# Sixteen-byte offsets for the operands of the matmuls

## The chip, the cores and the metric

The kernel runs on one core of a Trainium2 chip. The metric is the device time of one execution in microseconds. Three runs of the kernel before took 460.17 us in the median (460.16 to 460.78).

## The reference

Inputs are float32 q, k, v of shape (2, 12, 448, 64) and float64 weights, which arrive as pairs of 32-bit words. Cut to what is computed:

```python
scores = q @ k.transpose(0, 1, 3, 2) / sqrt(64)          # causal mask, softmax
x = (softmax(scores) @ v) -> (896, 768)                  # 2 batches x 448 tokens, 12 heads x 64
h = x @ w_in                                             # 768 -> 1024
solu = h * softmax(h)
y = layernorm(solu) * g_ln @ w_out                       # 1024 -> 768
out = relu(y @ moe2_w_in) ** 2 @ moe2_w_out              # 768 -> 2048 -> 768
```

## The kernel before

Every large product runs on TensorE in fp32r, with each operand split into a rounded part ("hi") and the remainder ("lo"); a product is three matmuls, hi x hi, hi x lo and lo x hi. TensorE loads 128 columns of one operand as weights (the second argument of `nc.tensor.matmul`) and streams the columns of the other (the third). The argument order in the listing is output, weights, moving operand; the profile prints the two inputs in either order.

The work is in five stages. Attention (to about 93 us, with a tail of L358 to 116 us) works head pair by head pair; its `pv` (L358) multiplies in plain fp32, with 448 and 64 or 320 and 192 columns, and one such matmul of the code shows as two instructions in the profile. Then h = x w_in (`h_part`, L474): for each of 7 token tiles and 6 channel blocks c, weights from x (`xT[c][s]`), moving operand from `W1[c]`, 512 columns. Then the layer norm, with transposes (L599), and y (`y_part`, L621): weights from `WO[fi]`, moving operand from `lnT`, for fi 0 to 7. Its first part (`y0`, order fi, then channel pairs cp) streams 384 columns; the second (`y1`, order cp, then fi) streams 512. For one fi and one cp there are 6 matmuls. Then y w_in2 (L752): weights from `W2[fi]`, moving operand from `yT[c][s]` in halves of 448 columns, 16 blocks of 36 matmuls. Last, the output product (L781): weights from `G[fi][s]`, moving operand from `W2[n]`, 384 columns, 16 blocks of 42 matmuls (two fi by 7 token tiles by 3).

The tiles that the change touches: `xT` and `yT` are the same 12 buffers (`xy_tiles`, L102, tags xy00 to xy51, c 0 to 5 and s 0 for hi, 1 for lo), 896 floats a partition. The output tiles `o` (L792) use 7 of those tags again. `G` (L719) is 32 tiles of 896 floats, for fi 0 to 15 and s 0 and 1. The weight buffers are handed out by `load_w` (L117) and `parts` (L127). `load_w` takes a buffer of a tag (w0, w1, w2 in one pool for blocks n modulo 3; the same three tags in a second pool, `wst`; wo0 to wo5 for `WO`) and loads the raw 64-bit words into it. `as_f32` (L139, three DVE instructions, L149 to L151) turns them into a float32 tile, and `parts` takes the same buffer again for hi (ACT, L674 in the last stages) and lo (POOL, L677). Three blocks ahead is loaded, two ahead is split: at the end of block n the load of block n+3 goes out, into the buffer that block n has freed.

The order of the work on each engine is written out by hand in `SEQ` for the stages up to y and by the loops from L747 on for the rest.

Where the buffers lie: every row length of these tiles is a multiple of 64 bytes (3584, 8192, 6144). In the compiled program all buffers of xy, w0 to w2 and `wst` begin at a multiple of 64 bytes within a partition; `lnT`, wo0 to wo5 and all of G begin 32 bytes past one. The slices that the matmuls take begin at multiples of 64 bytes within their tiles. So `WO[6]` and `WO[7]`, which lie in `wst`, begin at 0 modulo 64, and `WO[0]` to `WO[5]` at 32.

Of the kernel before, what the change touches and what calls it, by code (L numbers as in the profile page):

```python
# [7 lines left out]
F32 = mybir.dt.float32  # L8
F32R = mybir.dt.float32r
I32 = mybir.dt.int32  # L10
# [49 lines left out]
def attention_moe_kernel(tc, kq, v, w_in, w_out, g_ln, w_in2, w_out2, out):  # L60
# [7 lines left out]
    NP, P, _, S = kq.shape  # L68
    D = P // 2
    NT, DM = out.shape  # L70
# [5 lines left out]
    NF2 = DFF2 // P  # L76
# [7 lines left out]
    def pool(name, bufs=1, side="left", space=None):  # L84
        kw = {"space": space} if space is not None else {}
        return tc.tile_pool(name=name, bufs=bufs, side=side, reuse_waits="tile", **kw)

    def f(ap):
        return ap.bitcast(F32)

    with es:
        const = es.enter_context(pool("const"))
        xy = es.enter_context(pool("xy"))
# [5 lines left out]
        nhalf = const.tile([P, 1], F32, name="nhalf")  # L99
        nc.gpsimd.memset(nhalf, -0.5)  # L100

        def xy_tiles(nm):  # L102
            return [
                [xy.tile([P, NT], F32R, tag=f"xy{c}{s}", name=f"{nm}{c}{s}") for s in range(2)]
                for c in range(NC)
            ]

        xT = xy_tiles("xT")

        stage = ExitStack()  # L110
# [3 lines left out]

        wide = w_in.dtype != F32

        def load_w(pl, tag, src, W=2 * DFF, part=False):  # L117

            n = src.shape[1] if len(src.shape) < 3 + wide else src.shape[1] * src.shape[2]
            t = pl.tile([P, W], I32 if wide else F32, tag=tag, name="raw")  # L120
            d = t[:, 0 : 2 * n].rearrange("p (f t) -> p f t", t=2) if wide else t[:, 0:n]
            dd = d.rearrange("p (c f) ... -> p c f ...", c=src.shape[1]) if len(src.shape) > len(d.shape) else d
            if not part:
                nc.sync.dma_start(dd, src)
            return pl, tag, d, W

        def parts(w):  # L127

            pl, tag, d, W = w
            n = d.shape[1]  # L130
            t = pl.tile([P, W], F32R, tag=tag, name="w")
            return t[:, 0 : 2 * n].rearrange("p (s f) -> p s f", s=2)

        def words(w):
# [27 lines left out]
        def bank2(nm):  # L162

            pl = slots.pop(0)
            t = pl.tile([P, 2, 512], F32, tag="b", name=nm)
            slot_of[id(t)] = (pl, t)
            return t

        def give(t):
            slots.append(slot_of.pop(id(t))[0])  # L170
# [5 lines left out]
        with att:  # L176
# [7 lines left out]
            raw = qk_.enter_context(pool("raw", bufs=3, side="right"))  # L184
# [263 lines left out]
            def load_w1(c):  # L448
                W1[c] = load_w(w0 if c < 3 else wst, f"w{c % 3}", w_in[c * P : c * P + P, :])

            def load_w1_part(p):

                c, j = divmod(p, 4)
                src = w_in[c * P : c * P + P, :]
                if j == 0:
                    W1[c] = load_w(w0, f"w{c % 3}", src, part=True)
                n = DFF // 4
                nc.sync.dma_start(W1[c][2][:, n * j : n * j + n], src[:, n * j : n * j + n])
# [4 lines left out]
            def w1_hi(c):  # L463
                W1[c] = parts(W1[c])
                nc.scalar.copy(W1[c][:, 0], w_f[c])
# [71 lines left out]
            def load_wo(fi):  # L537
                pl, tag, W = (M["lnp"], f"wo{fi}", 2 * DM) if fi < NWO else (wst, f"w{fi - NWO}", 2 * DFF)
                WO[fi] = load_w(pl, tag, w_out[fi * P : fi * P + P, :], W)
# [4 lines left out]
            def wo_hi(fi):  # L544
                WO[fi] = parts(WO[fi])
                nc.scalar.mul(WO[fi][:, 0], w_f["o", fi], g_sb[:, fi : fi + 1])
# [95 lines left out]
            def y_out(cp, a):  # L642
                if not yT:
                    yT.extend(xy_tiles("yT"))
                b = (YB, YB1)[a].pop(cp)
                o, n = CH0 * a, (CH0, CH1)[a]
                for ci in range(2):
                    hi, lo = yT[2 * cp + ci]
                    nc.scalar.copy(hi[:, o : o + n], b[:, ci, 0:n])  # L649
                    nc.vector.tensor_tensor(lo[:, o : o + n], b[:, ci, 0:n], f(hi[:, o : o + n]), ALU.subtract)  # L650
                give(b)
# [20 lines left out]
            def w2_hi(n):  # L672
                W2[n] = parts(W2[n])
                nc.scalar.copy(W2[n][:, 0], w_f["2", n])  # L674
# [41 lines left out]
            moe0.close()  # L716
            gp = m2.enter_context(pool("gp", side="right"))
            tm = m2.enter_context(pool("tm", bufs=2))
            G = [[gp.tile([P, NT], F32R, name=f"g{fi}{s}") for s in range(2)] for fi in range(NF2)]  # L719
            HT = NT // 2  # L720
            rl = {}
            hb = {}
# [2 lines left out]
            def next_w2(n):  # L725

                if n + AHEAD < N2:
                    w2_f(n + AHEAD)
                    w2_hi(n + AHEAD)
                    w2_lo(n + AHEAD)  # L730
                if n + 3 < N2 and n + 3 >= NL2:
                    load_w2(n + 3)

            def relu_sq(fi):
# [4 lines left out]
                give(b)  # L739
                nc.scalar.copy(G[fi][0], rl[fi].rearrange("p a n -> p (a n)"))  # L740

            def relu_lo(fi):
                nc.vector.tensor_tensor(
                    G[fi][1], rl.pop(fi).rearrange("p a n -> p (a n)"), f(G[fi][0]), ALU.subtract
                )
# [21 lines left out]
            os_ = []  # L767
            for n in range(NF2, N2):
                half, fi = blocks2[n]
                if fi == 0:  # L770
                    bs = []
                last = fi == NF2 - TL
                for e, t in [(e, t) for t in range(NTT) for e in range(TL)] if last else [
                    (e, t) for e in range(TL) for t in range(NTT)
                ]:
                    if fi + e == 0 and t % 2 == 0:
                        bs.append(bank2("o"))
                    ob = bs[t // 2][:, t % 2, 0:HD]
                    hi, lo = (W2[n][:, s, HD * e : HD * e + HD] for s in range(2))
                    for s, w, r in ((0, hi, 0), (0, lo, 1), (1, hi, 2)):  # L780
                        nc.tensor.matmul(  # L781
                            ob,
                            G[fi + e][s][:, P * t : P * t + P],
                            w,
                            start=(fi + e == 0 and r == 0),
                            stop=(fi + e == NF2 - 1 and r == 2),
                        )
                    if not (last and e == TL - 1):
                        continue

                    if half == 0:
                        os_.append(xy.tile([P, NT], F32, tag=f"xy{t // 2}{t % 2}", name="o"))  # L792
                    if t % 2 or t == NTT - 1:
                        for t_ in range(t - t % 2, t + 1):
                            o = os_[t_][:, HD * half : HD * half + HD]
                            (nc.vector.tensor_copy if t_ % 2 else nc.scalar.copy)(o, bs[t // 2][:, t_ % 2, 0:HD])
                            nc.sync.dma_start(out[P * t_ : P * t_ + P, HD * half : HD * half + HD], o)
                        give(bs[t // 2])
                next_w2(n)
# [38 lines left out]
```

## Time and profile before

| What | us |
|---|---|
| Median of three runs | 460.17 |
| Span of the profiled execution | 459.8 |
| PE busy (matmuls) | 452.7 |
| PEld busy (weight loads) | 402.0 |
| DVE busy | 275.1 |
| ACT busy | 164.6 |
| POOL busy | 120.8 |

The span runs from the first to the last instruction of the profiled execution. A time of its own for that execution, from outside, is not among the runs listed; the runs give 460.16 to 460.78. PE and PEld are the two halves of TensorE, matmuls and loads of weights, and overlap. Matmuls are pipelined: an instruction lasts longer than the step to the next one, so the pace is the length of a block over its count, not the mean duration.

### The profile page before, as it was taken

Reading aid. Unit: us, or ns where it says so; the run is one execution under the profiler, and the core shown is the slowest. Engines: PE = TensorE matmul, PEld = TensorE weight load, DVE = VectorE, ACT = ScalarE, POOL = GpSimd, SP = SyncE. Lnnn points to the kernel's source line nnn. Section 1 sums busy time; section 2 is a strip of 40 time slices with the busy share of each in tenths; the row PEclk is TensorE's granted clock in tenths of the full one; section 3 lists DMA queues with packets and bytes.
Section 4 is the critical chain, followed back from the end, with each engine's and each line's share of the span. In section 5 each row is a group of like instructions: output and inputs, shape, how many; then the busy total and the mean of one; then the engine's idle time right before and its main releaser. Section 6 shows DMA issues by size and latency. Waiting matters only on the chain.

```text
span 459.8 us, 6525 instructions
## 1 busy us (share of the span) xinstructions
PE 452.7 (98%) x2535; PEld 402.0 (87%) x2535; DVE 275.1 (60%) x524; ACT 164.6 (36%) x213; POOL 120.8 (26%) x122
## 2 busy tenths in 40 slices
PE   8999899999999999999999999999999999999996
PEld 6777676787888899988899999999999999999996
DVE  8889687857569998741346566665763334342321
ACT  3465565533566636231133333424331010310101
POOL 3124547355321011110021322313122231222210
PEclk9999999999999999999999999999999999999999
DMA  8357765232173360000042423324243342734313
GB/s 251 128 154 221 207 159 164 62 79 98 41 280 133 96 248 2 0 1 0 0 138 69 138 80 127 116 91 137 70 137 80 128 113 94 240 90 135 86 52 120
DMA packets 41689, 52.47 MB, mean 114 GB/s; under 512 B 18234, under 2 KB 32314, under 8 KB 41274
## 3 DMA queue, kind: packets, MB, share of 16 engines
q1 hardware_dynamic: 41658, 52.05, 37.1%
q8 instruction: 20, 0.33, 0.3%
q14 instruction: 11, 0.09, 0.1%
HBM read 49.16 MB, written 2.80 MB: 113 GB/s over the span
## 4 chain that ended last, share of the span: by engine, by line
PE 93%; DMA 1%; POOL 1%; ACT 0%; issue 0%; SPq 0%; ACTq 0%; POOLq 0%
PE h L752 25%; PE o L781 25%; PE y L621 13%; PE h L474 13%; PE U L358 9%; PE s L317 4%; PE mxp L257 1%; DMA bc<-d 1%; PE T L599 1%; PE s L325 1%; POOL x L399 1%; PE mxp L284 0%; PE s L333 0%; ACT PP L349 0%; SPq L301 0%
## 5 line engine op out<-in xcount | busy, mean ns | idle before, releaser
L752 PE MATMUL h<-yT,w 128*128 128x448 f32 x576 | 116.9, 365 | 0.0
L781 PE MATMUL o<-w,g 128*128 128x384 f32 x672 | 116.8, 336 | 0.0
L781 PEld LDWEIGHTS o<-w,g 128*128 128x128 f32 x672 | 116.5, 188 | 0.3 <-DVE relu L738 0.2
L752 PEld LDWEIGHTS h<-yT,w 128*128 128x128 f32 x576 | 108.2, 188 | 8.6
L677 POOL TENSOR_TENSOR w<-wf,w 128x768 fp32r<-128x768 f32 x32 | 59.4, 1856 | 206.2 <-ACT w L674 206.2
L149 DVE TENSOR_SCALAR wf<-raw 128x768 int32<-128x768 int32 (+1 forms) x46 | 26.3, 573 | 83.6 <-DMA raw<-in_moe_w_out_dram 58.2
L674 ACT CAST w<-wf 128x768 fp32r<-128x768 f32 x32 | 26.8, 838 | 137.7 <-DVE wf L151 99.4
L474 PE MATMUL h<-w,xT 128*128 128x512 f32 x252 | 59.5, 393 | 0.0
L621 PE MATMUL y<-lnT,w 128*128 128x384 f32 (+1 forms) x288 | 58.9, 365 | 0.0
L621 PEld LDWEIGHTS y<-lnT,w 128*128 128x128 f32 x288 | 51.9, 188 | 5.9
L474 PEld LDWEIGHTS h<-w,xT 128*128 128x128 f32 x252 | 46.8, 188 | 9.6
L358 PE MATMUL U<-PP,VR 128*128 128x448 f32 (+1 forms) x192 | 49.2, 400 | 0.1
L151 DVE SCALAR_TENSOR_TENSOR wf<-raw,wf 128x768 int32<-128x768 int32 (+1 forms) x46 | 47.3, 1029 | 1.6
L150 DVE SCALAR_TENSOR_TENSOR wf<-raw,wf 128x768 int32<-128x768 int32 (+1 forms) x46 | 47.2, 1027 | 1.6
L358 PEld LDWEIGHTS U<-PP,VR 128*128 128x128 f32 x192 | 32.1, 190 | 16.4 <-issue 11.1
L399 POOL TENSOR_TENSOR x<-E,bc 64x448 f32<-64x448 f32 x24 | 31.9, 1328 | 47.2 <-DMA bc<-d 42.7
L272 DVE CUSTOM_DVE_ANT_0 JK<-mxp,MK 112x336 bf16<-112x336 f32 (+2 forms) x96 | 38.8, 446 | 8.5 <-PE mxp L257 7.5
L349 ACT ACTIVATE PP<-s 128x1024 f32<-128x1024 f32 x24 | 24.5, 1023 | 12.9 <-PE s L325 7.2
L738 DVE TENSOR_TENSOR relu<-h,relu 128x896 f32<-128x896 f32 x16 | 17.5, 1092 | 14.6 <-ACT relu L737 14.6
L346 POOL TENSOR_SCALAR_AFFINE_SELECT PP<-PP 128x256 f32<-128x256 f32 (+1 forms) x48 | 19.7, 443 | 21.3 <-ACT PP L349 20.8
L740 ACT CAST g<-relu 128x896 fp32r<-128x896 f32 x16 | 15.1, 942 | 18.6 <-DVE relu L738 18.6
L650 DVE TENSOR_TENSOR yT<-y,yT 128x384 fp32r<-128x384 f32 (+1 forms) x12 | 7.4, 624 | 22.7 <-ACT yT L649 22.7
(75 smaller groups left out, 349.3 us busy)
## 6 DMA issues: line engine op xcount, KB each, us to landing
raw<-in_moe_w_out_dram SPq DMA_DIRECT2D x24, 768.0 KB
raw<-in_moe_w_in_dram SPq DMA_DIRECT2D x16, 768.0 KB
r<-in_kq_dram SPq DMA_DIRECT2D x12, 448.0 KB
VR<-in_v_dram SPq DMA_DIRECT2D x12, 256.0 KB
raw<-in_moe_w_in_dram SPq DMA_DIRECT2D x12, 256.0 KB
raw<-in_moe_w_in_dram SPq DMA_DIRECT2D x3, 1024.0 KB
bc<-d SPq DMA_DIRECT2D x12, 224.0 KB
out_dram<-o SPq DMA_DIRECT2D x14, 192.0 KB
```

Of the source, the lines that this page charges most:

```text
L149: nc.vector.tensor_scalar(xi, hw, 3, 0x3FFFFFFF, ALU.logical_shift_left, ALU.bitwise_and)
L150: nc.vector.scalar_tensor_tensor(xi, hw, -0x40000000, xi, ALU.bitwise_and, ALU.bitwise_or)
L151: nc.vector.scalar_tensor_tensor(xi, lw, 29, xi, ALU.logical_shift_right, ALU.bitwise_or)
L272: nc.vector.tensor_tensor_reduce(JK[t], b[0:JP, h, o : o + nk], MK[:, S - nk :], 1.0, NEG, ALU.add, ALU.max, mx[i][:, 4 * h + t : 4 * h + ...
L358: nc.tensor.matmul(UB[i][:, h, q0:S], VR[i % 3][:, t, h, :], PP[(2 * i + a) % NPP][:, h, o : o + nq], start=t == 0, stop=t == 2,)
L399: nc.gpsimd.tensor_tensor(x[D * h : D * h + D], e[0:D, h], bc[:, h], ALU.mult)
L474: nc.tensor.matmul(b[:, half, :], xT[c][s][:, t * P : t * P + P], W1[c][:, w, 512 * half : 512 * half + 512], start=(c == 0 and s == 0 and ...
L621: nc.tensor.matmul(b[:, ci, 0:n], WO[fi][:, w, c * P : c * P + P], M["lnT"][a][s][:, fi, :], start=(fi == 0 and w == 0 and s == 0), stop=( ...
L674: nc.scalar.copy(W2[n][:, 0], w_f["2", n])
L677: nc.gpsimd.tensor_tensor(W2[n][:, 1], w_f["2", n], f(W2[n][:, 0]), ALU.subtract)
L752: nc.tensor.matmul(b[:, a, 0:HT], W2[fi][:, w, c * P : c * P + P], yT[c][s][:, HT * a : HT * a + HT], start=(c == 0 and w == 0 and s == 0) ...
L781: nc.tensor.matmul(ob, G[fi + e][s][:, P * t : P * t + P], w, start=(fi + e == 0 and r == 0), stop=(fi + e == NF2 - 1 and r == 2),)
```

## The change

Tiles of x, y and G and the weight buffers become 12 floats (48 bytes) longer in each partition, and a function `at` gives a window into them that begins 0, 4, 8 or 12 floats in (0, 16, 32 or 48 bytes). For x and y the place is (c + 2s) modulo 4, for G (fi + 2s) modulo 4, in units of 16 bytes. For weight buffers it goes by the last digit of the tag modulo 3: 0, 32 or 16 bytes for digits 0, 1 and 2. The raw words and the hi and lo parts of one block have the same place. The output tiles get the new length, since they share tags with x and y, but no offset.

```diff
+        def at(t, k, n):
+            o = 4 * (k % 4)
+            return t[:, o : o + n]
+
         def xy_tiles(nm):
             return [
-                [xy.tile([P, NT], F32R, tag=f"xy{c}{s}", name=f"{nm}{c}{s}") for s in range(2)]
+                [at(xy.tile([P, NT + 12], F32R, tag=f"xy{c}{s}", name=f"{nm}{c}{s}"), c + 2 * s, NT) for s in range(2)]
                 for c in range(NC)
             ]
...
+        def shift(tag):
+            return (0, 2, 1)[int(tag[-1]) % 3]
+
         def load_w(pl, tag, src, W=2 * DFF, part=False):
...
-            t = pl.tile([P, W], I32 if wide else F32, tag=tag, name="raw")
+            t = at(pl.tile([P, W + 12], I32 if wide else F32, tag=tag, name="raw"), shift(tag), W)
...
-            t = pl.tile([P, W], F32R, tag=tag, name="w")
+            t = at(pl.tile([P, W + 12], F32R, tag=tag, name="w"), shift(tag), W)
...
-            G = [[gp.tile([P, NT], F32R, name=f"g{fi}{s}") for s in range(2)] for fi in range(NF2)]
+            G = [[at(gp.tile([P, NT + 12], F32R, name=f"g{fi}{s}"), fi + 2 * s, NT) for s in range(2)] for fi in range(NF2)]
...
-                        os_.append(xy.tile([P, NT], F32, tag=f"xy{t // 2}{t % 2}", name="o"))
+                        os_.append(xy.tile([P, NT + 12], F32, tag=f"xy{t // 2}{t % 2}", name="o"))
```

## Rows read from the trace of the kernel before

**Rows 1.** The page's first part: busy us of each engine, share of the span.

```profile
PE 452.7 (98%) x2535; PEld 402.0 (87%) x2535; DVE 275.1 (60%) x524; ACT 164.6 (36%) x213; POOL 120.8 (26%) x122
```

**Rows 2.** PE by stretch: window and its length, busy (count), granted clock, DMA.

```profile
core 0: us, PE busy (x), PEclk, DMA share, GB/s
0.00:92.00 92.00, 88.54 (x642) 1.00 0.60 168
92.00:173.00 81.00, 81.00 (x399) 1.00 0.40 138
173.00:235.00 62.00, 62.00 (x312) 1.00 0.04 13
235.00:342.00 107.00, 107.00 (x532) 1.00 0.35 106
342.00:459.80 117.80, 114.17 (x658) 1.00 0.38 116
```

**Rows 3.** The page's fourth part: shares of the chain of waits by engine.

```profile
PE 93%; DMA 1%; POOL 1%; ACT 0%; issue 0%; SPq 0%; ACTq 0%; POOLq 0%
```

**Rows 4.** The chain of waits in order of time: start us, length us, what.

```profile
93.67 11.10 PE h L474 x48
...
108.11 1.73 PE U L358 x8
...
116.27 17.73 PE h L474 x78
...
162.14 15.60 PE y L621 x90
...
178.62 3.12 PE y L621 x18
...
182.62 3.17 PE y L621 x18
...
186.66 36.09 PE y L621 x162
222.75 116.74 PE h L752 x576
339.49 116.70 PE o L781 x672
...
456.21 0.48 ACT o L796
```

**Rows 5.** Weight loads by line: count, busy us, mean ns, idle before, releaser.

```profile
L781 PEld LDWEIGHTS o<-w,g 128*128 128x128 f32 x672 | 116.5, 188 | 0.3 <-DVE relu L738 0.2
L752 PEld LDWEIGHTS h<-yT,w 128*128 128x128 f32 x576 | 108.2, 188 | 8.6
```

**Rows 6.** L621's matmuls in stretches of its second part (512 columns), columns as rows 2.

```profile
189.39:197.55 8.16, 8.16 (x38) 1.00 0.00 0
197.79:200.59 2.80, 2.80 (x14) 1.00 0.00 0
200.59:208.75 8.16, 8.16 (x38) 1.00 0.01 2
208.75:211.55 2.80, 2.80 (x14) 1.00 0.00 0
211.55:219.71 8.16, 8.16 (x38) 1.00 0.00 0
```

**Rows 7.** Timeline of one L781 block: start, length, instruction, idle before and its releaser.

```profile
383.44 7.65 SPq L124 DMA_DIRECT2D raw<-in_moe_w_out_dram  x2
...
388.01 0.56 DVE L149 TENSOR_SCALAR wf<-raw 128x768 int32<-128x768 int32 x1 [4.59 <-DMA raw<-in_moe_w_out_dram]
...
390.72 0.84 ACT L674 CAST w<-wf 128x768 fp32r<-128x768 f32 x1 [6.31 <-PE o L781]
391.64 1.85 POOL L677 TENSOR_TENSOR w<-wf,w 128x768 fp32r<-128x768 f32 x1 [5.29 <-ACT w L674]
```

## Prediction

> **What bounds the kernel now.** I read the page's busy shares first: TensorE is busy 452.7 of 459.8 us, and its weight loads lie beside its matmuls [rows 1]. The granted clock is 1.00 in every stretch, which is the 2.4 GHz level [rows 2]. The chain of waits then says that nothing but TensorE matters: PE holds 93% of the chain [rows 3], and from 93.67 us to the last copy it is an unbroken series of matmul blocks [rows 4]. So this change counts by one thing: what it does to the time from one matmul's start to the next one's. What it does to DVE, ACT, POOL or a transfer counts only where PE would come to wait for it.
>
> That step comes out of the chain's blocks, length over count [rows 4]. L752 (448 columns): 116.74/576 = 202.7 ns. L781 (384): 116.70/672 = 173.7. L474 (512), in its long block: 17.73/78 = 227.3. L621 (384): 15.60/90 = 173.3. At 2.4 GHz a column takes 1/2.4 ns, so streaming alone is 186.7, 160.0, 213.3 and 160.0. The rest is a stall of 16.0, 13.7, 14.0 and 13.3 ns in each matmul. Over 576, 672, 252 and 288 matmuls that is about 26 us, and it is the whole stake.
>
> What is the stall? Each matmul streams one fp32r operand out of SBUF while the next matmul's 128 columns of weights load from SBUF as well (a load shows 188 ns, the length of a step [rows 5]). L358 has such loads too, at plain fp32: each of its matmuls shows as two instructions that take two cycles a column. Eight of them cover 2 x 2 x 512 columns, 1.707 us of streaming, and take 1.73 us [rows 4]: 2.9 ns each over. So a load beside a stream costs almost nothing when the stream asks at half rate, and 13 to 16 ns when it asks at full rate. I take the stall for a collision of the two reads.
>
> Does the place within 64 bytes matter to it? The kernel before has one contrast of its own, in L621. Its moving operand lies 32 bytes past a multiple of 64, its weights also 32 for fi 0 to 5, but 0 for fi 6 and 7. In the part with 512 columns the 36 steps of fi 0 to 5 take 8.16 us, 226.7 ns each, and the 12 steps of fi 6 and 7 take 2.80 us, 233.3 each, and it alternates so three times with no transfer running [rows 6]. (A row's count is two higher than the steps, because matmuls begun before the stretch are still draining.) In the part with 384 columns, 18 matmuls of fi 5 take 3.12 us and 18 of fi 6 take 3.17 us, 176.1 ns each [rows 4]. So a cheap step has a stall of 13.4 ns and a dear one 16.1 (384 columns) or 20.0 (512 columns). But the rows do not give a simple law: L781 has its moving operand at 0 and its weights at 32, also 32 apart, and pays 13.7; L752 has both at 0 and pays 16.0.
>
> [...]
>
> **The change part by part.** No instruction, wait, DMA or order is added or removed. *Longer tiles:* 48 bytes times 12 tiles of x and y, 32 of g and a dozen weight buffers; buffers only move. Cost 0. *Copies and subtractions that write shifted tiles* (DVE, ACT, POOL): no row shows one at an odd 16 bytes. In a block of L781 the last of this chain, POOL's subtraction, ends at 391.64 + 1.85 = 393.49, and PE wants that weight tile a block (42 x 173.7 = 7.30 us) after 390.72, at 398.02 [rows 7]. So 4.5 us of slack hide it; the chain from 388.01 is 5.5 us long and would have to grow by 80%. I take 0. *Loads into shifted buffers:* this one was issued at 383.44 and its data came by 388.01 [rows 7], 4.57 us. It may take twice as long before PE sees it. I take 0. *The output tile* is longer but not shifted: 0.
>
> *The matmul pairs.* The phases (address modulo 64) after it: x and y tiles take 16*((c+2s) mod 4), G the same with fi on top of 32, weight buffers 0, 32, 16 by tag. In L474, L752 and L781 the difference between a moving operand and the weights loading beside it thus runs over all four values: a quarter of the pairs at 0, a quarter 32 apart, half 16 or 48 apart. L621 gets equal phases for fi 0, 3, 7, 32 apart for fi 1, 4, 6 and 16 apart for fi 2 and 5.
>
> For unequal pairs the bounds are the cheap and the dear step. 32 apart has been both: dear in L621, cheap in L781; I take the middle. 16 or 48 apart has no row: from below, the stall of L358 (2.9 ns, a gain of some 11), from above the dear step; I again take the middle of cheap and dear, the rows nearest to it, and keep the gain as a rival. The middle is 1.4 ns above cheap at 384 columns (176.1 - 173.3 = 2.8, half) and 3.3 ns at 512 (6.6, half).
> - L781: three quarters of 672 = 504 x 1.4 ns = +0.71 us.
> - L474: three quarters of 252 = 189 x 3.3 = +0.62 us.
> - L621, 384 columns: five eighths of 144 = 90 x 1.4 = 0.13, less the 36 dear steps of today x 2.8 = 0.10: +0.03 us.
> - L621, 512 columns: 90 x 3.3 = 0.30, less 36 x 6.6 = 0.24: +0.06 us.
> - L752: pays 16.0 already at equal phases, between cheap and dear. Bounds: all cheap, 576 x (16.0 - 13.4) = -1.5 us; three quarters at the dear 20.0, 432 x 4.0 = +1.7 us. I take 0.
>
> Sum +1.4 us. The profiled execution spans 459.8 us; the median of the runs, 460.17, lies 0.4 above it, which I take for what lies around the span and leave as it is. **Forecast: 461.6 us**, slower by 0.3%. Its own range: 460.2 if every unequal pair stays cheap; with three quarters of all pairs dear L781 gives 1.4, L474 1.2, L621 0.5 and L752 1.7, together 4.8, so 465.0.
>
> **The rivals.**
> - *No effect.* For it: L781 pays the cheap stall 32 apart, so what L621 shows may belong to other address bits, or the collisions are only moved about within a step. Against it: the alternation in rows 6. Time 460.2.
> - *Faster: a difference of 16 or 48 bytes keeps the two reads out of each other's way.* Place: half of the pairs of L474, L752 and L781 and a quarter of L621's. If all of these came down to L358's 2.9 ns, L752 gains 288 x 13.1 = 3.8 us, L781 336 x 10.8 = 3.6, L474 126 x 11.1 = 1.4, L621 72 x 11 = 0.8: 9.6 us, 450.6. If only one of the two odd distances does it, 4.8 us: 455.4, which I give as this rival's time. It decides from 0.5 ns a matmul on (0.92 us over 1,788). For it: every operand now begins at 0 or 32, so no row excludes it, and the half-rate row shows that a load need not stall the stream. A small form is that L752 merely falls to the cheap stall: 458.7. Against it: the two reads advance along their rows, so a shift of the start may only change when they meet, not whether; cheap steps occur at equal phases and 32 apart alike. [...]
> - *Much slower.* Odd starts collide twice as often: half of the pairs pay another 13.4 to 16 ns, 288 x 16.0 + 336 x 13.7 + 126 x 14.0 + 72 x 13.4 = about 12 us: 472. No row speaks for it. A transfer into a buffer 16 bytes off that takes more than 9.1 us instead of 4.57 would also show here, as idle PE before blocks of L752 or L781.
>
> **How the numbers follow.** Forecast 0.46, no effect 0.19, faster 0.30, much slower 0.05. A measurement of this kernel tells about 0.2% from no change, 0.92 us. Of the forecast's share 0.38 lies above 461.1 and 0.08 below. So slower 0.43, within 0.2% 0.08 + 0.19 + 0.02 (of the rival's smallest form) = 0.29, faster 0.28. The range 454.5 to 465.0 leaves out the full gain (about 0.11) and the upper tail (0.06).
>
> **What would show it.** The chain's blocks after, length over count: L781 at about 174.7 ns, L474 above 230, L752 near 202.7, with the same 188 ns for a load. Within L752 the blocks of the three weight buffers, and within L781 the blocks of one phase of g, should differ from one another; if all have one pace, the phase does nothing. DVE, ACT and POOL durations should stand, and PE should have no new wait. I am wrong if L752 or L781 comes below its pace of today by 2 ns or more (then odd distances help), if all paces are as before, or if PE sits idle for a weight tile.

## The result and the profile after

The changed kernel takes 463.33 us in the median (462.88 to 463.64) against 460.17, a ratio of 1.0065 (95% interval 1.0052 to 1.0077): 3.2 us slower. The forecast was 461.6.

The first part of the page of the kernel after answers to [rows 1]: busy us by engine.

```profile
PE 455.6 (99%) x2535; PEld 403.1 (87%) x2535; DVE 275.0 (60%) x524; ACT 164.5 (36%) x213; POOL 120.6 (26%) x122
```

The other engines do the same work in the same time (DVE 275.1 before, ACT 164.6, POOL 120.8). The chain of waits of the kernel after answers to [rows 4]. Its line numbers are 7 higher: L481 was L474, L628 was L621, L759 was L752, L788 was L781. Columns: start us, length us, what.

```profile
92.04 11.33 PE h L481 x48
...
114.90 18.08 PE h L481 x78
...
161.49 15.69 PE y L628 x90
...
178.05 3.18 PE y L628 x18
...
182.10 3.18 PE y L628 x18
...
186.16 36.59 PE y L628 x162
222.74 117.03 PE h L759 x576
339.77 118.08 PE o L788 x672
...
457.88 0.48 ACT o L803
```

Every block of matmuls is the same work and a little longer. L788 takes 118.08 us for 116.70, +1.38. L759 takes 117.03 for 116.74, +0.29. The four pieces of L628 sum to 58.64 for 57.98, +0.66. The long piece of L481 goes from 17.73 to 18.08; over all its pieces L481 takes 58.66 us for 57.68, +0.98. Together +3.31 us, which is the whole loss (3.16 in the medians).

The two spans differ by only 1.6 us, and that needs a word. The profiled execution of before reached L474 at 93.67 us, the one of after reached L481 at 92.04: the attention stage, which the change does not touch, varies by this much from execution to execution (that of before had one wait of 1.5 us there, of PE in L317 for ACT's exponential). And in the runs made since, the time lies 1.8 us above the span, not the 0.4 that I took. So stages are compared by the lengths of their own blocks below, not by spans.

A block of L788, beside [rows 7]; columns as there.

```profile
376.88 7.76 SPq L131 DMA_DIRECT2D raw<-in_moe_w_out_dram  x2
...
381.56 0.56 DVE L156 TENSOR_SCALAR wf<-raw 128x768 int32<-128x768 int32 x1 [4.85 <-DMA raw<-in_moe_w_out_dram]
...
385.18 1.85 POOL L684 TENSOR_TENSOR w<-wf,w 128x768 fp32r<-128x768 f32 x1 [5.55 <-ACT w L681]
```

This is the block whose buffer is w2, shifted by 16 bytes: from the issue of its load to the first use of the data 4.68 us pass (4.71 for the same block before), and POOL's write of the shifted tile lasts 1.85 (1.85). The block of [rows 7] is the next one; its buffer is w0, whose window begins at 0, so it could not have shown a cost of the shift (4.41 for 4.57). What I costed at nothing on these engines cost nothing. The loss is all in the step from matmul to matmul.

### The profile page after: what moved, and what is told of

It reads as the page before. It is cut to its first block, busy times and chain, and to the rows that moved or that the text cites. A ratio compares the mean times of both kernels' runs of the same rounds, so it can differ in the third digit from the quotient of the medians.

```text
span 461.4 us, 6523 instructions
## 1 busy us (share of the span) xinstructions
PE 455.6 (99%) x2535; PEld 403.1 (87%) x2535; DVE 275.0 (60%) x524; ACT 164.5 (36%) x213; POOL 120.6 (26%) x122
## 4 chain that ended last, share of the span: by engine, by line
PE 94%; DMA 1%; ACT 1%; POOL 0%; issue 0%; SPq 0%; ACTq 0%; POOLq 0%
PE o L788 26%; PE h L759 25%; PE h L481 13%; PE y L628 13%; PE U L365 9%; PE s L324 4%; PE mxp L264 1%; PE T L606 1%; PE s L332 1%; DMA bc<-d 1%; POOL x L406 0%; PE mxp L291 0%; PE s L340 0%; ACT PP L356 0%; ACT xT L414 0%
## 5 line engine op out<-in xcount | busy, mean ns | idle before, releaser
L788 PE MATMUL o<-w,g 128*128 128x384 f32 x672 | 118.2, 337 | 0.0
L788 PEld LDWEIGHTS o<-w,g 128*128 128x128 f32 x672 | 117.8, 188 | 0.3 <-DVE relu L745 0.3
L759 PE MATMUL h<-yT,w 128*128 128x448 f32 x576 | 117.2, 365 | 0.0
L759 PEld LDWEIGHTS h<-yT,w 128*128 128x128 f32 x576 | 108.1, 188 | 9.0
L481 PE MATMUL h<-w,xT 128*128 128x512 f32 x252 | 60.5, 397 | 0.0
L628 PE MATMUL y<-lnT,w 128*128 128x384 f32 (+1 forms) x288 | 59.5, 367 | 0.0
L628 PEld LDWEIGHTS y<-lnT,w 128*128 128x128 f32 x288 | 52.1, 188 | 6.4
L481 PEld LDWEIGHTS h<-w,xT 128*128 128x128 f32 x252 | 46.8, 188 | 10.5
```

The costliest lines, as they stand in the source:

```text
L481: nc.tensor.matmul(b[:, half, :], xT[c][s][:, t * P : t * P + P], W1[c][:, w, 512 * half : 512 * half + 512], start=(c == 0 and s == 0 and ...
L628: nc.tensor.matmul(b[:, ci, 0:n], WO[fi][:, w, c * P : c * P + P], M["lnT"][a][s][:, fi, :], start=(fi == 0 and w == 0 and s == 0), stop=( ...
L759: nc.tensor.matmul(b[:, a, 0:HT], W2[fi][:, w, c * P : c * P + P], yT[c][s][:, HT * a : HT * a + HT], start=(c == 0 and w == 0 and s == 0) ...
L788: nc.tensor.matmul(ob, G[fi + e][s][:, P * t : P * t + P], w, start=(fi + e == 0 and r == 0), stop=(fi + e == NF2 - 1 and r == 2),)
```

## The experiments

In the diffs, `at(t, k, n)` is the window of n floats that begins 16k bytes into t. Steps are lengths of blocks over counts, or, where one buffer's blocks are told apart, the mean time from a start to the next start in the trace (a matmul itself lasts longer: 336 ns in L781 of the kernel before, at a step of 173.7). A stall is a step less 0.417 ns (1/2.4) a column. That pace is an estimate from the cheap steps of L621: 226.7 ns at 512 columns [rows 6] and 173.3 at 384 [rows 4], 53.4 ns for 128 columns, at a granted clock of 1.00 [rows 2]. The prediction's 2.4 GHz is the same number put as a clock; that a column takes one cycle of it is the author's estimate. For L358's two cycles a column the trace of the kernel before has 376 ns a step at 448 columns and 269 at 320 (medians), 0.836 ns a column, twice the other pace. Distances are (address of a matmul's moving operand minus address of the next matmul's weights, which load beside it) in the compiled programs.

**Constant shifts of the weight buffers.** The first question was whether the step depends on each pair's own phases, or on their changing.

```diff
-            t = pl.tile([P, W], F32R, tag=tag, name="w")
+            t = at(pl.tile([P, W + 12], F32R, tag=tag, name="w"), 1, W)   # w_const16; 2: w_const32; 3: w_const48
```

(The raw tile likewise.)

> All weight buffers begin 16 bytes in, nothing else is shifted, so every stage has one constant pair of phases. Theory A (settling): the stall falls to the cheap one wherever the phases stay the same from matmul to matmul, whichever they are; the changed kernel lost time because they change from step to step. Then L474 stays at 227 ns a step, L781 at 173.7, L752 at 202.7, and the time is 460.2 us, give or take 0.6. Theory B (own difference): each pair pays by the difference of its two phases as in the changed kernel's trace; then L474 pays 231, L781 174.8 to 175.3, L752 203.5, L621 176 and 232, and the time is about 463.

> All weight buffers begin 32 bytes in: L474 has its moving operand at 32 and its weights at 0, the pair that was dear in L621 before; L781 has both at 32; L621 has fi 0 to 5 at 32 and 0 (dear before) and fi 6 and 7 at 32 and 32 (cheap before). Theory A with no regard to which phases: all cheap, 460.2. Theory A with the one exception that the trace of before shows (moving 32, weights 0 never settles): L474 at 233 and L621 for fi 0 to 5 at 176.4 and 233, so +1.5 + 0.2 + 0.5 us, about 462.4. Theory B: the same for those, and L752 at 204 (32 apart) for another 0.9 us, 463.3.

> All weight buffers begin 48 bytes in. Theory A: cheap everywhere, L474 227, L781 173.7, L752 202.7, 460.2 us give or take 0.6. Theory B: L474 231, L781 175, L752 203, L621 176 and 232, about 462.8.

Measured: 464.41 us (ratio 1.0088, 1.0056 to 1.0119), 463.26 (1.0065, 1.0045 to 1.0086) and 464.33 (1.0084, 1.0052 to 1.0116). All are slower, so constant phases are not enough: theory A fell. But theory B did not hold either. The chain of w_const16:

```profile
222.67 117.52 PE h L756 x576
340.19 118.21 PE o L785 x672
```

L785 pays 175.9 ns a step in the mean, but its three weight buffers, all 48 bytes off within 64, differ: 179.6, 173.9 and 173.5 ns. The same is seen in w_const32. Here are three consecutive blocks of 36 steps of its L756 (window, its length, busy and count, clock, DMA):

```profile
267.54:274.75 7.21, 7.21 (x37) 1.00 0.34 109
274.75:282.11 7.36, 7.36 (x37) 1.00 0.35 107
282.11:289.50 7.39, 7.39 (x37) 1.00 0.34 109
```

That is 200.3, 204.4 and 205.3 ns, each steady through the block, with all three buffers at the same place within 64 bytes. In the kernel before the blocks are all alike. What differs between the three buffers is their place modulo 256 bytes: the longer rows are rounded up to 8256 bytes, 64 more than a multiple of 256. So the longer rows, which I had put at no cost, became the suspect.

**Only G shifted.**

```diff
-            G = [[gp.tile([P, NT], F32R, name=f"g{fi}{s}") for s in range(2)] for fi in range(NF2)]
+            G = [[at(gp.tile([P, NT + 12], F32R, name=f"g{fi}{s}"), fi + 2 * s, NT) for s in range(2)] for fi in range(NF2)]
```

> Only G is shifted, by fi and s as in the changed kernel; weight buffers, x and y are as before. Only L781 can move. In the changed kernel L781 lost 1.38 us (175.7 ns a step against 173.7). Theory A: alternation between hi and lo weights 32 bytes apart unsettles it: 175 to 176 ns, +0.9 to +1.5 us, 461.1 to 461.7. Theory B: the moving operand stays at 0, a quarter of the weights each at 0, 16, 32, 48; with the changed kernel's means for moving 0 (177.5, 174.9, 174.6, 175.9) the same +1.4 us. If instead only the changing moving phase matters, nothing: 460.2.

```profile
221.86 116.74 PE h L756 x576
338.60 118.29 PE o L785 x672
```

461.66 us (ratio 1.0028, 1.0014 to 1.0041). L785 loses 1.59 us and L756 nothing: this one edit costs that stage a little more than the whole change did (1.38). It does not tell A from B, nor offset from length.

**Length and offset apart.** Two runs share the change out. `longer_only` has all the 48-byte extensions and every offset at 0. `offsets_256` has the offsets of x, y and w0 to w2, with rows longer by 64 floats, so that nothing else moves modulo 256 (G and wo as before).

```diff
# longer_only: every at(...) of the change with k = 0
# offsets_256 (likewise the weight buffers w0 to w2, and the output tiles in length):
-                [xy.tile([P, NT], F32R, tag=f"xy{c}{s}", name=f"{nm}{c}{s}") for s in range(2)]
+                [at(xy.tile([P, NT + 64], F32R, tag=f"xy{c}{s}", name=f"{nm}{c}{s}"), c + 2 * s, NT) for s in range(2)]
```

> All tiles are longer by 48 bytes as in the changed kernel, but every window begins at 0, so all phases modulo 64 are those of the kernel before; the allocator rounds the rows up to 3648, 8256 and 6208 bytes, so the buffers move by steps of 64 against each other modulo 256. Theory C (the distance between the two streams modulo 256 bytes sets the settled step, and a distance that changes from matmul to matmul keeps it from settling): most of the loss comes back, L474 at 231 to 233 ns, L781 near 175, L752 202 to 204, and the time is 462 to 463. Theory D (only the place within 64 bytes counts): nothing is lost, 460.2.

> x, y and the weight buffers w0 to w2 get the offsets of the changed kernel, but their rows are longer by 256 bytes instead of 64, so that nothing else moves modulo 256; G and the wo buffers are as before. Theory C: the distances run over -48 to +48 bytes and change every one to three matmuls, so L474 does not settle, 231 to 233 ns (+1.0 us); L752 202 to 204; L781 has constant distances of 224, 240 and 256 bytes by buffer, which w_const16 and before show at 173.6, 179.6 and 173.9, so near 175.5 (+1.2 us); time 462 to 463. Theory that the rounding to 64 alone makes the loss: L474 227, L752 202.7, L781 173.7, 460.2 to 460.4.

`longer_only`: 463.40 us (ratio 1.0063, 1.0048 to 1.0077). `offsets_256`: 462.59 us (1.0049, 1.0036 to 1.0062). First the chain of `longer_only`, then of `offsets_256`:

```profile
115.89 18.00 PE h L478 x78
...
186.94 36.53 PE y L625 x162
223.46 116.90 PE h L756 x576
340.36 117.78 PE o L785 x672
```

```profile
114.73 18.03 PE h L481 x78
...
185.80 36.01 PE y L628 x162
221.81 117.10 PE h L759 x576
338.91 118.08 PE o L788 x672
```

The longer rows alone, with every phase modulo 64 as before, lose nearly all that the change loses: theory D (only the place within 64 bytes) is out. The offsets alone lose 2.1 us: in L481, L759 and L788 together 2.63 us, where the change lost 2.65, and nothing in L628, whose wo buffers they leave alone (36.01 for 36.09). Either way of disturbing the distances modulo 256 does it, and the two do not add up. In `offsets_256` the distances of L788 are constant for each weight buffer: 224, 240 and 0 bytes. Its steps are 173.8, 179.5 and 174.0 ns; w_const16 gave 179.6 for 240 too.

**A map of the distances.** If the distance modulo 256 sets the step, it can be read off by giving the three weight buffers of L752 and L781 three places.

```diff
+                W2[n] = load_w(w0, f"w{n % 3}", ..., k=(15, 14, 13)[n % 3])   # scan_a; scan_b: (12, 8, 4); rows W + 64
```

> A map of more distances. The three weight buffers of L752 and L781 begin 240, 224 and 208 bytes in (rows longer by 256), so L752's moving operand lies 16, 32 and 48 bytes past its weights and L781's 208, 192 and 176. If the distance modulo 256 bytes sets the settled step: three levels in each of L752 and L781, by buffer, constant within a buffer's blocks; from the short spells of L621 in the runs so far L781 at 173.3, 173.1 and 176.1, L752 between 200 and 207. If only the place within 64 bytes counts, L752 has 203 to 204 throughout.

> The same with 192, 128 and 64 bytes: L752's distance is 64, 128 and 192 bytes, L781's 160, 96 and 32. If the distance modulo 256 sets the step: L781 at 173.2, 176.6 and 175.9, L752 at three levels between 200 and 207. If only the place within 64 bytes counts: L752 202.7 and L781 173.7 in all blocks, as before.

One run each: 462.96 and 467.80 us. (In scan_b the attention stage took 7 us longer, as told in the last section; its L755 takes 116.40 us and its L784 117.33.) Three blocks of scan_a's L755:

```profile
266.01:273.34 7.33, 7.33 (x38) 1.00 0.36 107
273.34:280.77 7.43, 7.43 (x37) 1.00 0.33 106
280.77:288.12 7.35, 7.35 (x37) 1.00 0.36 109
```

Again three levels: 203.6, 206.4 and 204.2 ns in these blocks; over all blocks of each buffer 203.3, 206.7 and 204.1. With the runs above the map is whole. The mean step in ns in the blocks of one distance, by distance in bytes modulo 256:

| Distance | 448 columns (L752) | 384 columns (L781) | Distance | 448 columns | 384 columns |
|---|---|---|---|---|---|
| 0 | 202.7 | 173.9 | 128 | 204.0 | 176.1 |
| 16 | 203.3 | 175.6 | 144 | 204.0 | 175.0 |
| 32 | 206.7 | 173.4 | 160 | 200.1 | 173.3 |
| 48 | 204.1 | 173.9 | 176 | 203.3 | 176.0 |
| 64 | 200.2 | 173.3 | 192 | 202.4 | 173.3 |
| 80 | 206.7 | 175.0 | 208 | 202.1 | 176.5 |
| 96 | 205.4 | 176.6 | 224 | 204.4 | 173.7 |
| 112 | 202.2 | 173.5 | 240 | 206.6 | 179.6 |

No distance gets below a stall of 13.3 ns (173.3 less 160.0; 200.1 less 186.7 is 13.4), and the worst costs over 6 more. The kernel before sat at 0 in L752 and 224 in L781. For L781 my expectation missed two of the six distances: 208 bytes came out at 176.5 for 173.3, and 32 at 173.4 for 175.9. Those numbers came from spells of 18 steps in L621; the other four were as said.

This miss says more than that. In all runs of the map only one operand moved: in L781 G lay at 224 modulo 256 and the weight buffer varied, in L752 y lay at 192. That it is the distance, and not the place of the operand that varied, rests on distances that come back with other places. Some agree: 96 bytes at 384 columns gives about 176.6 ns with moving operand and weights at 32 and 192 (L621 before), 160 and 64 (L625 of w_const32) and 64 and 224 (L784 of scan_b). Others do not. Four spells of w_const48's L625 (384 columns; 18, 18, 18 and 17 steps at 16, 208, 80 and 16 bytes):

```profile
161.41:164.59 3.18, 3.18 (x18) 1.00 1.06 353
164.59:167.72 3.13, 3.13 (x20) 1.00 1.05 386
...
170.83:173.95 3.12, 3.12 (x19) 1.00 0.00 0
173.95:176.90 2.95, 2.95 (x18) 1.00 0.01 3
```

At 80 bytes the step is 173.3 ns for the table's 175.0, at 208 bytes 173.9 for 176.5. At 16 bytes it is 176.7 in the first spell and 173.5 in the last, steady in both, with both operands at the same places modulo 256. (Transfers run beside the first spell and not beside the last, but also beside the cheap second one.) So the table holds for the long blocks in which it was read; what else picks the step that a spell settles on stays open.

**Distances chosen.** Before the map was whole, 160 and 64 bytes were already known to be good.

```diff
-                W2[n] = load_w(w0, f"w{n % 3}", src.rearrange("(c p) f ... -> p c f ...", p=P))
+                W2[n] = load_w(w0, f"w{n % 3}", src.rearrange("(c p) f ... -> p c f ...", p=P), k=6)
-                WO[fi] = load_w(pl, tag, w_out[fi * P : fi * P + P, :], W)
+                WO[fi] = load_w(pl, tag, w_out[fi * P : fi * P + P, :], W, k=2 if fi >= NWO else 0)
# and rows of all weight buffers W + 64
```

> Distances chosen from the runs so far and kept constant: the weight buffers of L752 and L781 (but not of L474) begin 96 bytes in, with rows longer by 256 bytes, so that L752's moving operand lies 160 bytes past its weights modulo 256 and L781's 64; WO[6] and WO[7] begin 32 bytes in, so that they lie to lnT as WO[0] to WO[5] do. Theory C: L752 settles at 200.1 ns (-1.5 us), L781 at 173.3 (-0.2), L621's dear steps vanish (-0.3): 458.2 us, under both kernels. Theory B or D (only the place within 64 bytes): L752 32 bytes apart pays 203 to 204, L781 0 to -0.2, L621 -0.3: 460.0 to 460.7.

```profile
160.54 15.60 PE y L624 x90
...
181.01 3.13 PE y L624 x18
185.02 35.77 PE y L624 x162
220.79 115.23 PE h L755 x576
336.01 116.50 PE o L784 x672
```

458.13 us, ratio 0.9957 (0.9944 to 0.9970): faster than both kernels. L755 takes 115.23/576 = 200.1 ns a step, L784 173.4, and L624's dear steps of fi 6 and 7 are gone (3.13 for 3.17, 35.77 for 36.09). The expectation of theory C, 458.2, was made from the steps alone.

**Is it changing that costs?** In the changed kernel even pairs at a good distance pay: in L788 those at 0 pay 176.4 ns where 173.9 is the step of the map. Two runs let the distance alternate, by shifting G's lo tiles alone.

```diff
-            G = [[gp.tile([P, NT], F32R, name=f"g{fi}{s}") ...
+            G = [[gp.tile([P, NT + 64], F32R, name=f"g{fi}{s}")[:, 40 * s : 40 * s + NT] ...   # alternate_dear: 32 * s
```

> Only the lo tiles of G begin 160 bytes in, rows longer by 256. L781's moving operand then lies 224 bytes past the hi weights and 64 bytes past the lo weights, modulo 256. Kept constant, each of these distances settles at the cheap step: 173.7 ns (before) and 173.4 (placed). If alternation by itself keeps the step from settling: 175 to 176.5 ns, +1 to +2 us, 461.2 to 462.2. If each matmul pays by its own distance: 173.5 ns and 460.2 us.

> As in alternate, but the lo tiles of G begin 128 bytes in, so that L781's moving operand lies 224 bytes past the hi weights (settled step 173.7 ns when constant) and 96 past the lo weights (176.6 when constant, scan_b). Two steps of three have the hi weights beside them. If each step pays for its own distance alone: (2 x 173.7 + 176.6)/3 = 174.7 ns, 117.4 us for L781. If a dear step keeps its cheap neighbours from settling: steps beside hi weights come out above 173.7 too, L781 at 176 to 177 ns, 118.3 us or more.

First `alternate`, then `alternate_dear`:

```profile
338.68 116.66 PE o L781 x672
```

```profile
338.23 117.98 PE o L781 x672
```

`alternate` takes 460.79 us (ratio 1.0003, 0.9993 to 1.0013) and L781 173.6 ns a step: changing between these two good distances cost nothing, and that theory fell as well. `alternate_dear` takes 175.6 ns (one run, 461.63 us), between the two expectations. Its steps beside the hi weights, whose distance has not changed, rise from 173.7 to 176.0, and the dear steps fall from 176.6 to 174.6. So in this run a dear distance spoiled the steps of its good neighbours, by 2.3 ns in the mean: a step was not a sum over pairs.

**Is the stall a collision of reads?** This kernel, run once (452.32 us), leaves most of the reading out and keeps the counts.

```diff
-                                yT[c][s][:, HT * a : HT * a + HT],
+                                yT[c][s][:, HT * a : HT * a + 1].broadcast_to((P, HT)),
-                            G[fi + e][s][:, P * t : P * t + P],
+                            G[fi + e][s][:, P * t : P * t + 1].broadcast_to((P, P)),
```

> Leaves work out: L752 streams one column of y again and again (448 times) instead of 448 columns, and L781 loads one column of G 128 times as its weights. Counts and sizes of matmuls and loads are the same, only the addresses read are fewer. If the stall is a collision of the two reads of SBUF: L752 falls to 187 to 192 ns and L781 to 160 to 165. If it is a fixed price of changing weights in the array: 202.7 and 173.7 stay.

```profile
220.90 102.17 PE h L752 x540
...
333.22 113.65 PE o L781 x654
```

L752 falls to 102.17/540 = 189.2 ns, a stall of 2.5: with one column streamed again and again, a load of 128 different columns of weights beside it costs no more than that. L781 stays at 113.65/654 = 173.8, although its loads now read one column 128 times. So the stall goes when the moving operand stands still (from 16.0 ns to 2.5 in L752), and stays when only the load does (13.7 and 13.8 in L781). A fixed price of more than 2.5 ns for loading weights into the array is out, since L752 loads them in every step too. That is half of my account. That the load has a part in the stall is shown above the floor of 13.3 ns: in scan_a and scan_b only the weights of L755 moved, and its step went from 200.2 to 206.7. For the floor itself it is not shown, since no run streamed at full rate without loads. How a load of one column can still be in the way was not tried further.

## Why the prediction was right or wrong

- *What bounds the kernel, and where the effect lies:* right. All of the loss is in the steps of the four blocks; DVE, ACT, POOL, the loads and the waits of PE stood as costed.
- *Direction:* right: steps that were cheap became dear, as named, but in part by luck. The phases modulo 64, from which the sign was worked out, are those of the kernel before in `longer_only`, which by that count costs nothing and lost 2.9 us. *Size:* 1.4 us forecast, 3.2 measured, inside the forecast's own range (460.2 to 465.0), but more than twice the sum.
- *The term that was mis-sized:* the price of the unequal pairs. I let equal pairs keep the cheap step and the others pay the middle of cheap and dear: L781 +0.71, L474 +0.62, L621 +0.09, L752 0. Measured: +1.38, +0.98, +0.66, +0.29. In L628 with 512 columns all distances pay 230 to 234 ns, equal phases too.
- *The step behind it that failed:* "Longer tiles: buffers only move. Cost 0." `longer_only` costs 2.9 us by itself. I had reduced addresses modulo 64 because every tile was a multiple of 64 long, and read the contrast of [rows 6] as "32 apart". It was, but modulo 256: fi 6 and 7 lay 96 bytes apart in the 384-column part and 32 in the other, both dear in the map or in the rows, while L781's "32 apart" was 224, which is cheap. The contradiction that the prediction noted between these two rows was the sign of it.
- *No effect:* the map does not agree, with 200.1 to 206.7 ns in L752's matmuls by address alone.
- *Faster by odd offsets:* wrong in its place. No distance of 16 or 48 bytes is under the cheap step. Its small form, L752 falling to the cheap stall for 1.5 us, exists at a distance of 64 or 160 bytes and is what `placed` collects. The floor of a stream without collision, 2.9 ns by L358, was right: one_column shows a stall of 2.5 ns in L752.

## What to carry to other kernels

Where a stage is a gapless run of full-rate matmuls (0.417 ns a column here, and the stall), divide the block's length by its count and compare blocks that differ only in where their buffers lie. If they differ, write down each operand's address modulo 256 bytes, since padding a row moves every buffer behind it (48 bytes more cost 2.9 us in `longer_only`); keep the distance between the moving operand and the weights constant and at a value that the trace shows to be cheap (`placed`: 458.13 us, L752's step 200.1 ns), or mix cheap ones only (one such mix was tried: `alternate`, 173.6 ns in L781). Time it in the block itself: the step of a short spell did not always carry over to a long one (208 bytes: 173.3 ns in spells of L621, 176.5 in L781's blocks). Spreading the buffers over all places cost 3.2 us here: it met dear distances, and in `alternate_dear` such a distance raised its neighbours' steps from 173.7 to 176.0 ns.

## What the runs showed of the hardware

- In these runs the step of fp32r matmuls with a weight load each went with where the two operands lie modulo 256 bytes in SBUF: in long blocks at one distance 200.1 to 206.7 ns at 448 columns, 173.3 to 179.6 at 384. Distance alone did not fix it (w_const48's spells at 16 bytes: 176.7 and 173.5).
- At the head of L474 in the kernel before the cheap step came only after some steps: the first ones are 335, 224, 231, 236, 228, 232 and 231 ns from start to start, and then 226 to 227 holds.
- The attention stage varies without any edit. In scan_b it ended about 7 us later than in the other runs. Its first matmuls of L361 show it, in scan_b's chain:

```profile
21.77 3.38 PE U L361 x8
...
27.41 1.92 PE U L361 x8
```

The two groups stream the same number of columns (448 and 64, then 320 and 192), in 3.38 us at first and 1.92 later. The same group of matmuls that fill idle time, in scan_b (L506) and in the kernel before (L503):

```profile
7.83 1.86 PE L506 MATMUL fill<-Z 128*128 128x448 f32 x4
```

```profile
7.52 1.00 PE L503 MATMUL fill<-Z 128*128 128x448 f32 x4 [0.29 <-DVE mx L272]
```

From start to start such a matmul of 448 columns takes 373 ns at first in every run, 1.2 columns a ns, and 192 to 194 later. The granted clock is shown as 1.00 throughout, but the trace's record of it begins only at 24.35 us in scan_b and at 3.96 to 6.44 us in the other runs. So in scan_b TensorE kept the longer step for 18 to 20 us more, although it was busy for 18.90 of the first 20 us. Why the shorter step came so late there stays open.
